# Delta-rule attention, gated MLP and rotor MLP on one core: a reordered end of the first block inversion, fused small steps, early TensorE products, rank offsets

## The chip, the cores and the metric

The kernel runs on one core of a Trainium2 chip. The metric is the device time of one execution in microseconds.

## The reference

Three layers run one after another on batch 4, sequence 768, width 384 (8 heads of 48).

```python
# 1. delta rule, per batch and head, t = 0 .. 767
y[t]  = q[t] @ state
state = state + beta[t] * outer(k_n[t], v[t] - k_n[t] @ state)   # k_n = k / (norm(k) + 1e-6)
# 2. gated MLP: h = relu(x @ w_in); u, v = halves of h; v normalised over its width
x = (u * (w_spatial @ v_n + b_spatial)) @ w_out
# 3. rotor: theta = x @ w_theta
u = x + w_tok_r @ (x * cos(theta)) + w_tok_i @ (x * sin(theta))
out = u + relu(u @ w_ch)
```

## The kernel before, in words

**Chunks.** The delta rule runs in chunks of 64 tokens: 12 chunks for each of 4 batches, 48 chain steps g. A chain step (chain, L865) turns the state S of all 8 heads into the next one: line 888 multiplies keys and state, line 891 subtracts, line 900 multiplies by the chunk's inverse (in tile GX), copies make U, line 914 adds to the state in PSUM, line 943 makes the outputs. jit (L816) makes the masked query-key products (L833, L839) and scales v by the key norms.

**Rounds.** The inverse of a chunk's unit-triangular 64x64 matrix is made for 8 chunks at once, a round, of 32 units (chunk and pair of heads): gram2 (L656) makes the key products (L677), one call for two chunks, and invert (L695) inverts. invert(0) is on the way to the first chain step; its tasks are marked crit. It transposes the 32x32 diagonal blocks into tile un (L717), takes the norms from their diagonal (L721 to L730), scales (L734), and then substitutes backwards, k from 30 to 1: for every k a product into tmp (L756) and an addition to un (L767). In round 0 the rows are split into an even and an odd set, so that there are four instructions for a k; in later rounds two. At k = BURSTK = 8 of round 0 a task on TensorE (L761) waits for tmp, and 60 transposes of the identity (filler, L553 to L556) follow it: the burst. Then come a scaling (L770), a transpose (L773), a transpose into GX (L776), two copies within GX (L530), two GpSimd fills of zeros (L783), and, for 8, 8 and 16 units, the products that make the off-diagonal block: L794, copies out of PSUM into ct, L800, copies out of PSUM into GX (all copies go through the helper's lines L524 on ScalarE and L530 on VectorE). L800 of the first 8 units reads GX's right half, which the copies of all 32 units write.

**The rest.** The MLP's products are all on line 1055 (tiles m and y), three products of rounded halves for each one; their weights are loaded as 8-byte numbers and turned into 4-byte ones by ScalarE and VectorE (L970 to L986).

**What sets the order.** Every piece of work is a task in a list, with the engines that it may run on, a planned duration, a rank (prio) and what it needs. Plan.run (L297) plays the list through a model of the chip and issues each engine's instructions in the order that comes out; each engine works its queue in that order. The rank of a chain step is g, that of its neighbours g plus or minus a few. Where the model sees TensorE idle for a stretch, it puts transposes of the identity (fill, L556) ahead of the next task, some 0.6 of the planned gap, or as many as the model of the clock asks for, at most 16. NUDGE holds runs of tasks by number, whose ranks get a random offset from a seed; it is empty.

## Time and profile before

| | us |
|---|---|
| median of 3 runs (719.7 to 723.13) | 722.24 |
| the profiled execution | 721.76 |
| its span, first to last instruction | 720.0 |
| TensorE busy | 683.0 |
| VectorE busy | 549.6 |
| ScalarE busy | 360.5 |

How to read it: a busy time is the union of an engine's instructions. A matmul's recorded duration contains its way through the array, so matmuls one behind another overlap in the record, and the distance of two starts is what one costs. "Idle before" names what ended the wait of an engine.

### The profile page before, as it was taken

Reading aid. Unit: us, or ns where it says so; the run is one execution under the profiler, and the core shown is the slowest. Engines: PE = TensorE matmul, PEld = TensorE weight load, DVE = VectorE, ACT = ScalarE, POOL = GpSimd, SP = SyncE. Lnnn points to the kernel's source line nnn. Section 1 sums busy time; section 2 is a strip of 40 time slices with the busy share of each in tenths; the row PEclk is TensorE's granted clock in tenths of the full one; section 3 lists DMA queues with packets and bytes.
Section 4 is the critical chain, followed back from the end, with each engine's and each line's share of the span. In section 5 each row is a group of like instructions: output and inputs, shape, how many; then the busy total and the mean of one; then the engine's idle time right before and its main releaser. Section 6 shows DMA issues by size and latency. Waiting matters only on the chain.

```text
span 720.0 us, 23423 instructions
## 1 busy us (share of the span) xinstructions
PE 683.0 (95%) x9801; PEld 629.2 (87%) x9801; DVE 549.6 (76%) x1576; ACT 360.5 (50%) x904; POOL 12.3 (2%) x22
## 2 busy tenths in 40 slices
PE   4597888999999999999999999999999999999998
PEld 4586777788887888888898999999999999999997
DVE  6998999999979989977666668967466745674555
ACT  4855575573286662387746854753243324431331
POOL 0010010010010010010000000000000000000000
PEclk9996976999999999999999999999999999999999
DMA  8533652534657335767696563521111111111001
GB/s 293 179 109 95 189 156 79 175 105 135 207 177 227 109 95 151 209 206 225 185 323 206 156 199 130 163 73 30 66 30 30 30 67 31 30 31 66 0 1 66
DMA packets 74121, 90.63 MB, mean 126 GB/s; under 512 B 7328, under 2 KB 58912, under 8 KB 74016
## 3 DMA queue, kind: packets, MB, share of 16 engines
q1 hardware_dynamic: 74016, 89.14, 40.2%
q8 instruction: 77, 1.26, 0.8%
q14 instruction: 28, 0.23, 0.1%
HBM read 66.70 MB, written 22.41 MB: 124 GB/s over the span
## 4 chain that ended last, share of the span: by engine, by line
PE 77%; DVE 14%; ACT 4%; DMA 3%; issue 3%; SPq 0%; DVEq 0%; ACTq 0%
PE m L1055 40%; PE y L1055 22%; DVE un L767 3%; DVE tmp L756 3%; PE gp L556 3%; PE gp L800 2%; PE ru L943 2%; PE ru L900 1%; PE ru L888 1%; PE s L914 1%; PE gp L794 1%; DMA kq<-in_kqT_dram 1%; PE m L1366 1%; DVE un L773 1%; ACT ct L524 1%
## 5 line engine op out<-in xcount | busy, mean ns | idle before, releaser
L1055 PE MATMUL m<-w,vh 128*128 128x384 f32 x384 | 102.2, 347 | 0.0
L1055 PE MATMUL y<-wr,xTh 128*128 128x384 f32 x432 | 87.1, 339 | 0.0
L1055 PE MATMUL y<-w,xTl 128*128 128x384 f32 x432 | 86.3, 337 | 0.0
L1055 PEld LDWEIGHTS y<-wr,xTh 128*128 128x128 f32 x432 | 75.6, 188 | 0.1
L1055 PEld LDWEIGHTS y<-w,xTl 128*128 128x128 f32 x432 | 75.5, 188 | 0.0
L1055 PEld LDWEIGHTS m<-w,vh 128*128 128x128 f32 x384 | 66.7, 188 | 2.5
L1055 PE MATMUL m<-w,vl 128*128 128x384 f32 x192 | 64.4, 335 | 0.0
L756 DVE TENSOR_TENSOR tmp<-un 128x30 f32<-128x30 f32 (+21 forms) x209 | 60.9, 303 | 1.4
L767 DVE TENSOR_TENSOR un<-un,tmp 128x30 f32<-128x30 f32 (+21 forms) x209 | 61.0, 303 | 1.2
L1391 DVE TENSOR_SCALAR bgr<-m 128x384 int32<-128x384 f32 x22 | 12.3, 558 | 57.1 <-PE m L1055 56.8
L524 ACT ACTIVATE U<-ru 128x96 f32<-128x96 f32 x86 | 16.7, 247 | 57.6 <-PE ru L900 50.1
L1055 PE MATMUL m<-wo,gh 128*128 128x384 f32 x176 | 44.7, 334 | 0.0
L1055 PE MATMUL m<-xTh,wih 128*128 128x256 f32 x144 | 44.2, 307 | 0.2 <-ACT hv L524 0.2
L524 ACT ACTIVATE x<-m 128x384 f32<-128x384 f32 x22 | 10.6, 480 | 66.9 <-PE m L1055 66.9
L1055 PE MATMUL m<-xTl,wih 128*128 128x256 f32 x144 | 40.6, 282 | 0.0
L1055 PE MATMUL m<-xTh,wil 128*128 128x256 f32 x144 | 40.6, 282 | 0.0
L1055 PE MATMUL m<-uh,wc 128*128 128x384 f32 x144 | 39.2, 335 | 0.0
L524 ACT ACTIVATE bgr<-bgr 128x384 uint8<-128x384 uint8 x34 | 36.8, 1084 | 0.4
L1055 PEld LDWEIGHTS m<-w,vl 128*128 128x128 f32 x192 | 36.0, 188 | 0.0
L524 ACT ACTIVATE gh<-graw 128x256 fp32r<-128x256 f32 x27 | 10.0, 412 | 49.2 <-PE m L1055 47.5
L1055 PE MATMUL m<-wt,xh 128*128 128x384 f32 x132 | 33.8, 337 | 0.0
L943 PE MATMUL ru<-jp,U 64*64 64x64 f32 x768 | 33.2, 227 | 0.0
(186 smaller groups left out, 1669.0 us busy)
## 6 DMA issues: line engine op xcount, KB each, us to landing
kq<-in_kqT_dram SPq DMA_DIRECT2D x48, 256.0 KB, 3.6
vk<-in_vkn_dram SPq DMA_DIRECT2D x48, 192.0 KB, 3.3
kg<-in_kgT_dram SPq DMA_DIRECT2D x24, 256.0 KB, 3.6
gd<-gt SPq DMA_DIRECT2D x32, 192.0 KB, 3.2
xd<-xs SPq DMA_DIRECT2D x48, 96.0 KB, 3.2
xr<-xd SPq DMA_DIRECT2D x24, 192.0 KB, 3.3
bgr<-in_w_r_dram SPq DMA_DIRECT2D x12, 384.0 KB, 4.0
bgr<-in_w_i_dram SPq DMA_DIRECT2D x12, 384.0 KB, 4.1
```

What stands on the lines that cost most here:

```text
L524: nc.scalar.activation(out=out, in_=in_, func=func, **kw)
L556: nc.tensor.transpose(out, ident.t, ident.t)
L756: nc.vector.tensor_tensor(out=t3, in0=un.t[:, k:k + 1, 0:k].to_broadcast([128, m, k]), in1=un.t[:, t0:32:st, k:k + 1].to_broadcast([128, m ...
L767: nc.vector.tensor_tensor(out=un.t[:, t0:32:st, 0:k], in0=un.t[:, t0:32:st, 0:k], in1=t3, op=ALU.add)
L773: A([("DVE", 2080.0)], lambda e: nc.vector.transpose(out=un.t.rearrange("p u s -> p s u"), in_=un.t.rearrange("p t s -> p s t")), ub, [xt, ...
L794: mm(out=pv[q + 32:q + 64, u, :], lhsT=gx[q:q + 32, u0 + u, 32:64], rhs=un.t[q:q + 32, u0 + u, :], start=True, stop=True, tile_position=(q ...
L800: mm(out=pv[q:q + 32, u, :], lhsT=ct.t[q + 32:q + 64, u, :], rhs=gx[q + 32:q + 64, u0 + u, 32:64], start=True, stop=True, tile_position=(q ...
L888: mm(out=at(ps.t, RB[hp])[o:o + 64], lhsT=kq.t[a:a + D, 0, hp, :], rhs=s[a:a + D, D * SB[hp]:D * SB[hp] + D], start=True, stop=True)
L900: mm(out=at(pu.t, UB[hp])[o:o + 64], lhsT=gx[i:i + 64, j * HP + hp, :], rhs=rt.t[i:i + 64, hp, :], start=True, stop=True)
L943: mm(out=PYv[h]()[o:o + 64, c0:c0 + CH], lhsT=lh, rhs=rh, start=f, stop=w == 1 or UF[hp] > 0, skip_group_check=True)
L1055: mm(out=view(), lhsT=a, rhs=c, start=(start and q == 0 and s_ == 0), stop=(stop and q == tot - 1 and s_ == 2))
L1391: P.add(o_dve(DM), lambda e: nc.vector.tensor_scalar(out=ni.t.bitcast(I32), in0=th(), scalar1=1.0 / TWO_PI, scalar2=None, op0=ALU.mult), [ ...
```

## The change

Norms: the sum and its scaling become one instruction that makes twice the norm, the factor -1 becomes -4, and the halving that the v scaling needs comes later. Substitution: for k from 26 and up to 3 in round 0 (from 28 and up to 2 in later rounds) each row, or column, of the step is one instruction, which multiplies by a scalar from un and adds. Round 0's transpose into GX, copies and GpSimd fills are made for the first 8 units and then for 24. The second group of 8 units gets the rank -19.6 + 0.3 in place of 0.75, the third 1.3 in place of 1.0. A GpSimd fill of a 128x128 tile and eight products of it with itself come first on their engines. NUDGE gets seven runs of tasks. A few constants are only written in another way.

```diff
@@ -89,12 +89,15 @@
 CTN = 1
 XRN = 2
 UPER = 6
+P2H = (0.3, 1.3)
+NWARM = 8
+KLO0, KHI0, KLO, KHI = 3, 26, 2, 28
 LZ = 0.0
 LZY = 0.0
 LZG = 1
 GAPY = 0
 STAY = 350.0
-NUDGE = ()
+NUDGE = ((758, 332, 362, 1.5), (9389, 1357, 1417, 0.1), (4962, 2530, 2590, 1.5), (5968, 2293, 2323, 0.1), (8329, 1405, 1525, 0.6), (9243, 2216, 2336, 1.5), (2589, 2425, 2675, 0.1))
 SPER = 3
 GTN = 3
 TPR = 3
@@ -635,6 +638,15 @@
         A([("POOL", 100.0)], lambda e, i=i: nc.gpsimd.memset(St[i][:, HP * D:], 0.0), (), SS[i], -30 + i, port=False)
         A([("POOL", 100.0)], lambda e, i=i: nc.gpsimd.memset(Ut[i][:, HP * D:], 0.0), (), UU[i], -30 + i, port=False)
 
+    warm = single("const", "warm", [128, 128])
+    A([("POOL", 150.0)], lambda e: nc.gpsimd.memset(warm.t, 0.0), (), [warm], -59.0, port=False)
+
+    def fw(e):
+        for _ in range(NWARM):
+            mm(out=RUt[:, 0, 128:256], lhsT=warm.t, rhs=warm.t, start=True, stop=True)
+
+    A(o_pe(230.0 * NWARM), fw, [warm], [], -59.0, act=0.95, mode=0)
+
     kq_b, vk_b, jp_b = {}, {}, {}
     ng_b = {}
     inv0, grams, first = [], [], []
@@ -697,7 +709,6 @@
         gx, G = GXt[r % NB], GXc[r % NB]
         cr = r == 0
         gg = [Buf(tile_=gx) for _ in range(4)]
-        gz = [Buf(tile_=gx) for _ in range(4)]
         gm2 = [Buf(tile_=gx)]
         for u0, u1 in ((0, 16), (16, 24), (24, 32)) if cr else ((0, 32),):
             for q in (1, 3):
@@ -722,12 +733,11 @@
         A([("ACT", 120.0)], lambda e: act(sr.t, ss.t, ACTF.Sqrt), [ss], [sr], pr, crit=cr)
         for f in (lambda e: V.reciprocal(out=nt.t, in_=sr.t),
                   lambda e: V.tensor_tensor(out=nt.t, in0=nt.t, in1=ss.t, op=ALU.mult),
-                  lambda e: V.tensor_tensor(out=nt.t, in0=nt.t, in1=sr.t, op=ALU.add),
-                  lambda e: V.tensor_scalar(out=nt.t, in0=nt.t, scalar1=0.5, scalar2=1e-6, op0=ALU.mult, op1=ALU.add)):
+                  lambda e: V.scalar_tensor_tensor(out=nt.t, in0=sr.t, scalar=2e-6, in1=nt.t, op0=ALU.add, op1=ALU.add)):
             A(o_dve(32), f, [ss, sr], [nt], pr, crit=cr)
         for f in (lambda e: V.reciprocal(out=gt.t, in_=nt.t),
                   lambda e: V.tensor_tensor(out=gt.t, in0=gt.t, in1=gt.t, op=ALU.mult),
-                  lambda e: V.scalar_tensor_tensor(out=gt.t, in0=gt.t, scalar=-1.0, in1=beta_sb.t[:, 32 * r:32 * r + 32], op0=ALU.mult, op1=ALU.mult)):
+                  lambda e: V.scalar_tensor_tensor(out=gt.t, in0=gt.t, scalar=-4.0, in1=beta_sb.t[:, 32 * r:32 * r + 32], op0=ALU.mult, op1=ALU.mult)):
             A(o_dve(32), f, [nt, beta_sb], [gt], pr, crit=cr)
 
         def f2(e):
@@ -735,6 +745,7 @@
             nc.vector.memset(dg(), 1.0)
 
         A([("DVE", d_dve(1024) + 160.0)], f2, [gt], [un], pr, crit=cr)
+        A(o_dve(32), lambda e: V.tensor_scalar(out=nt.t, in0=nt.t, scalar1=0.5, scalar2=None, op0=ALU.mult), [gt], [nt], pr + 0.001)
         A(o_dve(32), lambda e: V.transpose(out=ng.t.rearrange("p j h -> p (j h)"), in_=nt.t), [nt], [ng], pr + 0.001, port=False)
 
         sets = [(0, 1)] if not cr else [(0, 2), (1, 2)]
@@ -742,6 +753,16 @@
         fin = [[] for _ in sets]
         heads = []
         for k in range(30, 0, -1):
+            if k <= (KLO0 if cr else KLO) or k >= (KHI0 if cr else KHI):
+                def fs(e, k=k):
+                    for x in range(k + 1, 32) if k > 15 else range(k):
+                        o, i, c = ((un.t[:, x, 0:k], un.t[:, k, 0:k], un.t[:, x, k:k + 1]) if k > 15 else
+                                   (un.t[:, k + 1:32, x], un.t[:, k + 1:32, k], un.t[:, k, x:x + 1]))
+                        nc.vector.scalar_tensor_tensor(out=o, in0=i, scalar=c, in1=o, op0=ALU.mult, op1=ALU.add)
+
+                n = 31 - k if k > 15 else k
+                A([("DVE", n * d_dve(31 - n))], fs, [un], ub, pr + 0.001 * (31 - k), crit=cr).order.update(heads[-3:])
+                continue
             for half in (0, 1):
                 for i, (c0, st) in enumerate(sets):
                     t0 = k + 1 + (k + 1 - c0) % st
@@ -773,20 +794,29 @@
         A([("DVE", 2080.0)], lambda e: nc.vector.transpose(out=un.t.rearrange("p u s -> p s u"),
                                                            in_=un.t.rearrange("p t s -> p s t")),
           ub, [xt, un], pr + 0.05, crit=cr, port=False)
-        A([("DVE", 1163.0)], lambda e: nc.vector.transpose(out=gx[:, :, 0:32], in_=un.t), [xt, un], gg, pr + 0.1, crit=cr, port=False)
-        if cr:
-            inv0.append(P.tasks[-1])
-        for q in (1, 3):
-            A(o_cps(1024), lambda e, q=q: copy(e, gx[32 * q:32 * q + 32, :, 32:64], gx[32 * q:32 * q + 32, :, 0:32]),
-              [], [gg[q]], pr + 0.2, crit=cr, part=32 * q)
-        for q in (1, 3):
-            A([("POOL", 890.0)], lambda e, q=q: nc.gpsimd.memset(gx[32 * q:32 * q + 32, :, 0:32], 0.0),
-              [gg[q]], [gz[q]], pr + 0.3, crit=cr, port=False)
+        parts = []
+        for n, (a0, a1) in enumerate(((0, 8), (8, 32)) if cr else ((0, 32),)):
+            ga, za = [Buf(tile_=gx) for _ in range(4)], [Buf(tile_=gx) for _ in range(4)]
+            parts.append((a0, a1, ga, za))
+            w, p0 = a1 - a0, pr + (0.1 if n == 0 else 0.6)
+            A([("DVE", 50.0 + 34.8 * w)], lambda e, a0=a0, a1=a1: nc.vector.transpose(out=gx[:, a0:a1, 0:32], in_=un.t[:, a0:a1, :]),
+              [xt, un] + gg, ga, p0, crit=cr, port=False)
+            if cr:
+                inv0.append(P.tasks[-1])
+            for q in (1, 3):
+                A(o_cps(32 * w), lambda e, q=q, a0=a0, a1=a1: copy(e, gx[32 * q:32 * q + 32, a0:a1, 32:64], gx[32 * q:32 * q + 32, a0:a1, 0:32]),
+                  [], [ga[q]], p0 + 0.01, crit=cr, part=32 * q)
+            for q in (1, 3):
+                A([("POOL", 60.0 + 26.0 * w)], lambda e, q=q, a0=a0, a1=a1: nc.gpsimd.memset(gx[32 * q:32 * q + 32, a0:a1, 0:32], 0.0),
+                  [ga[q]], [za[q]], p0 + 0.02, crit=cr, port=False)
         u0 = 0
         for h, mu in enumerate((8, 8, 16) if cr else (16, 16)):
             ps, ct = r_gp.new(), r_ct.new()
             pv = GPt[:, 256:256 + mu * 32].rearrange("p (a b) -> p a b", b=32)
-            p2 = pr + 0.5 + 0.25 * h
+            p2 = pr + 0.5 + 0.25 * h if not cr or h == 0 else P2H[h - 1]
+            near = [x for x in parts if x[0] < u0 + mu and u0 < x[1]]
+            gd = [x[2][q] for x in near for q in (1, 3)]
+            zd = [x[3][q] for x in near for q in (1, 3)]
 
             def f2(e, pv=pv, u0=u0, mu=mu):
                 for u in range(mu):
@@ -804,13 +834,13 @@
             for q in (1, 3):
                 A(o_cpp(32 * mu), lambda e, q=q, pv=pv, ct=ct, mu=mu: copy(e, ct.t[32 * q:32 * q + 32, 0:mu], pv[32 * q:32 * q + 32]),
                   [ps], [(ct, True)], p2, crit=cr, port=False, part=32 * q)
-            A(o_pe(525 * mu // 8), f3, [ct, gg[1], gg[3]], [(ps, True)], p2, crit=cr, act=0.46, mode=3)
+            A(o_pe(525 * mu // 8), f3, [ct] + gd, [(ps, True)], p2, crit=cr, act=0.46, mode=3)
             if cr and h == 1:
                 first.append(P.tasks[-1])
             for q in (0, 2):
                 A(o_cpp(32 * mu), lambda e, q=q, pv=pv, u0=u0, mu=mu: copy(e, gx[32 * q:32 * q + 32, u0:u0 + mu, 32:64],
                                                                     pv[32 * q:32 * q + 32]),
-                  [ps, gg[1], gg[3], gz[1], gz[3]], [G[i] for i in range(u0 // HP, (u0 + mu) // HP)], p2, crit=cr, port=False, part=32 * q)
+                  [ps] + gd + zd, [G[i] for i in range(u0 // HP, (u0 + mu) // HP)], p2, crit=cr, port=False, part=32 * q)
             u0 += mu
 
     def jit(g, pr):
```

## Rows read from the trace of the kernel before

**Rows 1.** Windows by stage: engine busy us, TensorE clock, DMA share, GB/s.
```profile
0.00:31.00 31.00, 14.24 (x401) 12.40 (x402) 24.68 (x115) 21.29 (x51) 0.44 (x8) 1.00 0.82 274
...
55.00:140.00 85.00, 73.95 (x1830) 61.56 (x1829) 78.39 (x264) 48.58 (x148) 1.89 (x2) 0.78 0.47 136
140.00:500.00 360.00, 356.85 (x5870) 320.14 (x5859) 295.62 (x848) 208.90 (x530) 8.07 (x10) 1.00 0.55 168
```

**Rows 2.** Windows: the two long stretches at half clock.
```profile
54.97:68.63 13.66, 10.27 (x226) 9.01 (x229) 10.46 (x46) 7.09 (x21) 0.00 (x0) 0.50 0.25 72
...
99.35:119.83 20.48, 17.95 (x416) 14.44 (x412) 18.46 (x56) 11.93 (x28) 1.67 (x2) 0.50 0.26 76
```

**Rows 3.** The burst's transposes, two stretches: ns min/median/max, first and last start.
```profile
L556 PE MATMUL gp<-ident x15: 421/421/421, 31.2 to 34.2; 128*128 128x128 f32 x15
...
L556 PE MATMUL gp<-ident x52: 272/273/337, 34.4 to 40.0; 128*128 128x128 f32 x52
```

**Rows 4.** Timeline of TensorE, gram calls: start us, us, engine, line, form.
```profile
4.14 1.13 PE L677 MATMUL gp<-kg 48*64 48x64 f32 x32 [4.14 <-DMA kg<-in_kgT_dram]
...
71.31 0.66 PE L677 MATMUL gp<-kg 48*64 48x64 f32 x32
```

**Rows 5.** Timeline of VectorE, first inversion.
```profile
13.38 0.18 DVE L726 TENSOR_SCALAR nT<-nT 128x32 f32<-128x32 f32 x1
...
15.96 0.29 DVE L756 TENSOR_TENSOR tmp<-un 128x30 f32<-128x30 f32 x2
...
16.74 0.34 DVE L756 TENSOR_TENSOR tmp<-un 128x28 f32<-128x28 f32 x2
16.99 0.33 DVE L767 TENSOR_TENSOR un<-un,tmp 128x28 f32<-128x28 f32 x2
...
18.29 0.38 DVE L756 TENSOR_TENSOR tmp<-un 128x75 f32<-128x75 f32 x2
...
33.69 0.32 DVE L756 TENSOR_TENSOR tmp<-un 128x42 f32<-128x42 f32 x2
...
35.17 1.23 DVE L770 TENSOR_TENSOR un<-un,gaT 128x1024 f32<-128x1024 f32 x1
...
38.59 1.25 DVE L776 STREAM_TRANSPOSE GX<-un 128x1024 f32<-128x1024 f32 x1
```

**Rows 6.** Timeline of TensorE, 31 to 47 us.
```profile
31.17 9.32 PE L556 MATMUL gp<-ident 128*128 128x128 f32 x69
40.42 0.69 PE L794 MATMUL gp<-un,GX 32*32 32x32 f32 x32
...
43.05 0.69 PE L800 MATMUL gp<-GX,ct 32*32 32x32 f32 x32
...
46.19 0.45 PE L900 MATMUL ru<-rt,GX 64*64 64x48 f32 x16
```

**Rows 7.** Groups by form on VectorE: count, busy us, mean ns, idle before.
```profile
L1398 DVE TENSOR_SCALAR bgm<-bgm 128x384 f32<-128x384 f32 x24 | 8.6, 358 | 0.6
...
L1131 DVE TENSOR_SCALAR hv<-hv,mv,td 128x512 f32<-128x512 f32 x14 | 7.3, 542 | 0.0
```

**Rows 8.** Timelines of ScalarE and VectorE: copies behind lines 794, 800.
```profile
41.56 1.06 ACT L524 ACTIVATE GX<-GX 32x1024 f32<-32x1024 f32 x1
43.79 0.76 ACT L524 ACTIVATE GX<-gp 32x256 f32<-32x256 f32 x2 [1.17 <-PE gp L800]
...
41.57 0.43 DVE L530 COPY ct<-gp 32x256 f32<-32x256 f32 x1 [1.01 <-ACT ct L524]
```

**Rows 9.** Chain of work that ended last: waits without a releaser.
```profile
53.38 2.62 issue
...
97.37 1.02 issue
...
304.76 1.45 issue
```

**Rows 10.** Windows, transposes of line 556 alone, 140 to 500 us.
```profile
140.00:500.00 360.00, 6.88 (x48) 5.22 (x48) 1.00 0.55 168
```

More of the change, by code (lines that the diff above doesn't have):

```diff
@@ L37 @@
 FILL_ACT = 0.6
-FILL_LOW = .5
+FILL_LOW = 0.5
 FILL_K = 16
@@ L59 @@
 HAM_DN = 0.44
-HAM_T = .42
+HAM_T = 0.42
 SLIDE = 3413
```

## The prediction

> **What bounds the kernel now.** First I read the stretches [rows 1]: from 140 to 500 us TensorE is busy 356.85 of 360 us, before 31 us 14.24 of 31, between 55 and 140 us 73.95 of 85. So the late part is TensorE's own work, and whatever starts this work sooner ends the kernel sooner; what can be lost or won lies before 140 us. Then the granted clock: two long stretches there are at 0.50, the lower level of 1.2 GHz [rows 2]. Before 34 us the profile prints 1.00, but the rows say otherwise: the burst of transposes starts 15 of them between 31.2 and 34.2, one per 0.214 us, and 52 between 34.4 and 40.0, one per 0.11 us [rows 3], so the clock was at its lower level until some 3.2 us into the burst, and a gram call takes 1.13 us at 4.14 where it takes 0.66 at 71.31 [rows 4].
>
> Then VectorE up to 40 us [rows 5]. It is the chain there: the substitution begins at 15.96 and ends at 35.17, then scaling, one transpose, another from 38.59, copies. The reader should see how small instructions follow one another: a pair of 128x28 takes 0.25 us from start to start (16.74 to 16.99), 0.125 each, although one lasts 0.18.
>
> Last TensorE from 31 us [rows 6]. The burst (60 transposes and 9 that the planner adds as fill) holds it until 40.42; the first products of the finishing steps (line 794) start there, though their operand was ready when VectorE began the next transpose at 38.59. So TensorE's queue, not VectorE, is last at this point, by about 1.85 us. Fill, line 800 at 43.05, more fill, and the first chain step's line 900 at 46.19 follow.
>
> **The change, part by part.** All against the profiled execution: span 720.0, its own time 721.76, which is 0.48 below the median of 722.24.
>
> *Norms.* One of four dependent small steps goes. The scaling on line 726 takes 0.18 us [rows 5]. The halving returns behind the last use and falls into the gap before the substitution, for about half a step, as does the small transpose that used to lie in a gap. I take -0.1; bounds -0.18 and +0.1.
>
> *Fused steps, k from 30 to 26.* Before, 18 instructions from 15.96 to 18.29: 2.33 us [rows 5]. After, 15 instructions of 26 to 30 elements, each row's next update at least two instructions behind the one it needs. At 0.125 each that is 1.88: -0.45. The trace has no such instruction with a scalar from memory at this size. The nearest is line 1131 [rows 7]: 128x512 with two such scalars takes 542 ns where a plain 128x384 on line 1398 takes 358; scaled by its elements the plain one would be near 0.43, so the scalars may cost 0.12. Bounds: 0.1 each gives -0.83, 0.24 each gives +1.3. I take the pair's rate, since its elements and type are those of the change.
>
> *Fused steps, k from 3 to 1.* Before 33.69 to 35.17, 1.48 us; after, 6 instructions at 0.125 and two waits of about 0.11 for the column just written: 0.97. This 0.5 us I cost at nothing: the burst covers it, since TensorE is 1.85 us late there. If that cover went, it would count in full. In the five later inversions three pairs of steps trade places with as many fused ones, with TensorE full: nothing.
>
> *The burst and its fill.* The burst is released by the k = 8 step, behind the first two edits and ahead of the third, so it moves by 0.55. The fill of 9 is set from the planned gap between burst and line 794; VectorE's planned work in that gap shrinks, so I estimate 6 in place of 9. At 0.11 us each [rows 3]: -0.3. Bounds: none left (-1.0) and twice as many (+1.0).
>
> *The eight products.* In the code a gram call has 16 products and the trace shows 32 matrix instructions for it [rows 4], so eight products of full size are 16 instructions; at the burst's slow 0.214 us they last 3.4 us. Released by a small GpSimd fill at about 1 us (an estimate: VectorE's and GpSimd's first fills all lie before that), they end near 4.5, where the first gram now starts at 4.14. So they may hold the grams by up to 0.5 us; or, being as long as what came ahead of the clock's rise in the burst, raise it, and a gram then takes 0.66 in place of 1.13 [rows 4], which is worth up to 0.5 on VectorE's way to the substitution. I take 0, with both ends. The Trainium skill (TensorE: Matmul & The Clock Gate, Part 4: PE-mode transpose) says that transposes do not engage the full clock; by that rule the burst would be useless and the products alone could lift the clock, and the sum would be about 0.5 better; the rate that doubles inside the burst [rows 3] disagrees, and no trace here shows the products.
>
> *The last steps for 8 units first.* Now line 800 needs the copy into the right half of all 32 units, which ScalarE does from 41.56 to 42.62, behind its first copy out of PSUM [rows 8]; VectorE's copy out of PSUM ends at 42.0; line 800 starts at 43.05 behind fill. After, transpose, copies and GpSimd fills for 8 units are a quarter as long and end before the burst does, so line 800 is held by the PSUM copies alone: 42.0 in place of 43.05, -1.05. From the end of the last copies (43.79 plus 0.76, [rows 8]) to line 900 at 46.19 pass 1.64 us: a mask's product, fill and the next units' line 794, all set ahead of it. With chain steps 0 and 1 ready earlier and the remaining 24 units ranked behind, I take about half, -0.9; bounds 0 and -1.64. What is late next: TensorE's order, then VectorE, where the 24 units' transpose and copies now stand among the PSUM copies. The weight conversions on VectorE that wait for the transpose into GX now wait for its second part; they are behind it on the same engine anyway, at no cost.
>
> These parts bring the first chain step 0.1 + 0.45 + 0.3 + 1.05 + 0.9 = 2.8 us forward; with TensorE full after 140 us it arrives at the end.
>
> *A wait that has no cause in the data.* At 53.38 TensorE stands for 2.62 us in the middle of line 800, with no releaser in the profile; five other waits of over a microsecond without one stand on the chain, none above 1.5; the first and the last of the five are 1.02 and 1.45 [rows 9]. The 16 new instructions, the lost fill and the new order put another instruction there. I take a wait of some 1.1 us in its place, -1.5; bounds 0 and -2.62, or more if the clock does not fall behind it (below).
>
> *Rank offsets.* One run of tasks belongs to chain step 2 and what stands around it, six to the stretch of about 250 to 400 us. The first run also moves three loads on SyncE's queue (a gram's keys, and keys and values three steps ahead), which nothing waits for within the step. The latter can win at most the idle 3.15 us [rows 1] and the 6.88 us of fill [rows 10] between 140 and 500, and lose as easily. I take -0.5; bounds -5 and +3, estimates of about half of those 10 us and the idle time.
>
> Sum: -2.8 - 1.5 - 0.5 = -4.8; 721.76 - 4.8 = 717.0 us.
>
> **Rivals.** *Better: the first slow stretch goes too.* It begins at 54.97, 1.6 us into the wait at 53.38. Without that wait it may not come. It holds 10.27 us of TensorE work at half clock [rows 2], so at most 5.1 us; with the wait's other 1.1 us and some of it being fill, about 4.5: 717.0 - 4.5 = 712.5. For it: the cause is one wait. Against: the clock falls again at 99.35, with no such wait ahead of it on the chain but 1.02 us [rows 9]. Chance 0.2.
>
> *Lost in the queue.* The burst and the fill keep line 794 near 40 us, fused instructions cost what a scalar from memory may cost, and the order behind eats the rest; then only 1 us is left: 720.8. For it: TensorE is already later than VectorE. Against: line 800's hold is a plain wait that goes. That the early products do nothing at all belongs here. Chance 0.26.
>
> *Slower: another fall of the clock.* The place is 79 to 99 us, now at the full level; ranks of step 2 and its neighbours are shuffled by up to 1.5, and one idle stretch of TensorE as long as that at 53.38 would decide it. The price is that of the stretch at 99.35: 17.95 us of work at half clock, at most 9 us [rows 2]: 717.0 + 9 = 726. Chance 0.12.
>
> **How the numbers follow.** The forecast has 0.42. About half a per cent, 3.6 us, is what a measurement of this kernel tells from no change: below 718.6 is faster, above 725.9 slower. The forecast's own spread, 714 to 720, lies mostly below 718.6 (0.36), the better case wholly (0.2), of the queue case hardly anything (0.01): faster 0.57. Slower is the last rival, 0.12; the same 0.31. The range goes from 709, which leaves out the lower end of the better case, to 724, which takes in the queue case and leaves out the fall of the clock.
>
> **What would show it.** Right: line 794 starts at about 39.6, line 800 some 1.6 us behind it, line 900 of step 0 near 43.4; the fused instructions 0.125 us apart; TensorE's busy share from 140 us on unchanged. Wrong: a fused instruction every 0.2 us or more; burst and fill that end after 40.4; line 900 still behind 45 us; a granted clock of 0.50 in a stretch that now has 1.00; the wait without cause of 2 us or more at another place.

## The result, and the profile after

The changed kernel takes 730.39 us (median of 4 runs, 726.99 to 732.72) against 722.0 of the kernel before on the same chip: a ratio of 1.0117, interval 1.0093 to 1.0141. It is slower, by 8.4 us where 4.8 less were forecast, and above the range's 724. Its four executions fall into 727 to 728 us at a mean granted clock of 0.951 to 0.955 and 732 to 733 at 0.941 to 0.942; the profiled one took 728.38.

The page of the changed kernel (busy us, share, instructions; the clock in 40 slices; one transfer queue):

```profile
span 726.6 us, 23354 instructions
...
PE 682.7 (94%) x9767; PEld 626.1 (86%) x9767; DVE 552.1 (76%) x1574; ACT 362.0 (50%) x895; POOL 12.3 (2%) x25
...
PEclk7586798999999999998999999999999999999999
...
q8 instruction: 77, 1.26, 0.8%
```

TensorE is as busy as before (683.0 us then), so the 6.6 us that the span grew are time in which it stands. The stretches of [rows 1], and two more, say where:

```profile
0.00:31.00 31.00, 16.75 (x416) 14.84 (x416) 23.71 (x105) 19.46 (x47) 0.58 (x9) 0.66 0.82 269
31.00:55.00 24.00, 19.12 (x326) 17.22 (x327) 17.85 (x59) 9.74 (x24) 2.08 (x4) 0.78 0.19 54
55.00:140.00 85.00, 69.06 (x1833) 56.25 (x1835) 81.48 (x272) 49.78 (x141) 1.90 (x2) 0.84 0.50 142
...
300.00:345.00 45.00, 42.66 (x962) 35.33 (x961) 32.86 (x95) 29.36 (x74) 1.89 (x2) 0.92 0.61 187
...
140.00:500.00 360.00, 354.63 (x5904) 315.52 (x5905) 293.74 (x842) 209.19 (x523) 7.71 (x10) 0.99 0.56 168
...
323.90:330.71 6.81, 6.47 (x96) 5.13 (x95) 4.16 (x9) 3.60 (x8) 0.00 (x0) 0.50 0.24 66
```

The same stretches of the kernel before that were not shown:

```profile
31.00:55.00 24.00, 21.43 (x456) 19.47 (x457) 22.15 (x72) 12.55 (x29) 1.89 (x2) 1.00 0.28 86
...
300.00:345.00 45.00, 44.70 (x1057) 36.92 (x1056) 35.47 (x98) 33.49 (x88) 1.90 (x2) 1.00 0.69 209
```

TensorE's idle time goes from 16.76 to 14.25 us before 31, from 2.57 to 4.88 up to 55, from 11.05 to 15.94 up to 140, and from 3.15 to 5.37 from 140 to 500: together 6.9 more. Idle time is not all loss, since fill gave way to it (200 transposes of line 556 before, 150 of line 559 after), so I also counted the 2,808 products of the MLP (line 1055 before, 1085 after) along the trace. After 360 of them the next starts at 222.4 before and 221.8 after, after 600 at 304.6 and 301.6: by this count the changed kernel is up to 3 us ahead. After 720 the next starts at 341.7 and 344.6, after 1,200 at 428.5 and 435.1. The count is rough, because chain work between the products changes places with them; but a lead that turns into 6.6 us of delay says that the end is lost between 300 and 430 us. There, and at the start, in the timeline of TensorE:

```profile
0.99 3.78 PE L646 MATMUL ru<-warm 128*128 128x128 f32 x16 [0.99 <-POOL warm L642]
...
6.79 0.69 PE L689 MATMUL gp<-kg 48*64 48x64 f32 x32 [0.16 <-DVE GX L701]
...
10.05 1.13 PE L689 MATMUL gp<-kg 48*64 48x64 f32 x32 [1.88 <-DMA kg<-in_kgT_dram]
...
32.08 0.48 PE L782 MATMUL gp<-ident,tmp 128*128 128x128 f32 x1 [2.71 <-DVE tmp L777]
33.03 8.77 PE L559 MATMUL gp<-ident 128*128 128x128 f32 x60 [0.47 <-ACT GX L527]
...
42.97 0.69 PE L824 MATMUL gp<-un,GX 32*32 32x32 f32 x32
...
46.62 0.69 PE L830 MATMUL gp<-GX,ct 32*32 32x32 f32 x32 [1.71 <-ACT ct L527]
...
49.24 0.68 PE L930 MATMUL ru<-rt,GX 64*64 64x48 f32 x16
...
324.24 0.49 PE L973 MATMUL ru<-jp,U 64*64 64x64 f32 x7 [2.34 <-issue]
```

The last row is a new wait that nothing in the profile releases, 2.34 us from 321.90 in the middle of line 973. From 323.90 to 330.71 the granted clock is at its lower level of 1.2 GHz: 6.47 us of work that takes about half as long at the upper one, 3.2 us lost. The two together are 5.6 us, against the 6.6 us by which the span grew. In the kernel before the stretch from 300 to 345 us holds 0.30 us of idle time and no fall.

The start is late too, and for other reasons. Line 824 is line 794 of before, 830 is 800 and 930 is 900 [rows 6]: 42.97 for 40.42, 46.62 for 43.05, 49.24 for 46.19. ScalarE's timeline:

```profile
11.23 0.66 ACT L527 ACTIVATE GX<-gp 128x256 f32<-128x256 f32 x2 [1.03 <-PE gp L689]
11.91 1.28 ACT L527 ACT_TABLE_LOAD   x1
13.21 0.23 ACT L527 ACTIVATE sr<-ss 128x32 f32<-128x32 f32 x1
...
41.84 0.38 ACT L527 ACTIVATE GX<-gp 128x256 f32<-128x256 f32 x1 [8.86 <-PE gp L559]
42.25 2.13 ACT L527 ACTIVATE GX<-GX 32x1024 f32<-32x1024 f32 x2
44.41 0.94 ACT L527 ACTIVATE w<-gt 128x384 fp32r<-128x384 f32 x2
45.37 0.41 ACT L527 ACTIVATE GX<-GX 32x256 f32<-32x256 f32 x1
45.80 0.76 ACT L527 ACTIVATE ct<-gp 32x256 f32<-32x256 f32 x2
```

The reader should see the order in the queue. The second copy of the last gram out of tile gp (41.84) stands behind the burst, which writes the same tile; it waits 8.86 us. Line 824 is held by the end of burst and fill; behind the copy stand 3.07 us of other work, and only then the copy for the 8 units (45.37) and the one into ct (45.80), which line 830 waits for. And at 11.23 two gram copies and the table load of 1.28 us stand ahead of the square root, which starts at 13.21 where it started at 12.28 before.

VectorE:

```profile
13.47 0.35 DVE L734 RECIPROCAL nT<-sr 128x32 f32<-128x32 f32 x1 [1.08 <-ACT sr L527]
...
16.50 0.25 DVE L761 SCALAR_TENSOR_TENSOR un<-un 128x30 f32<-128x30 f32 x1
...
16.79 2.67 DVE L761 SCALAR_TENSOR_TENSOR un<-un 128x29 f32<-128x29 f32 x14
...
19.54 0.38 DVE L777 TENSOR_TENSOR tmp<-un 128x75 f32<-128x75 f32 x2
...
34.99 1.45 DVE L761 SCALAR_TENSOR_TENSOR un<-un 128x28 f32<-128x28 f32 x6
```

The 14 fused instructions take 2.67 us, 0.19 each. From the first step to k = 25 pass 3.04 us; before 2.33 [rows 5]. From the first of the six at the end of the substitution to the scaling behind them (36.47) pass 1.48, as before (33.69 to 35.17).

### The profile page after: what moved, and what is told of

Same layout as the page of the kernel before. It is cut to its first block, busy times and chain, and to the rows that moved or that the text cites. A ratio compares the mean times of both kernels' runs of the same rounds, so it can differ in the third digit from the quotient of the medians.

```text
span 726.6 us, 23354 instructions
## 1 busy us (share of the span) xinstructions
PE 682.7 (94%) x9767; PEld 626.1 (86%) x9767; DVE 552.1 (76%) x1574; ACT 362.0 (50%) x895; POOL 12.3 (2%) x25
## 4 chain that ended last, share of the span: by engine, by line
PE 70%; DVE 20%; ACT 4%; issue 3%; DMA 2%; DVEq 0%; POOL 0%; ACTq 0%; SPq 0%; POOLq 0%
PE m L1085 36%; PE y L1085 22%; DVE un L788 4%; DVE tmp L777 4%; PE gp L824 2%; PE gp L559 1%; PE ru L930 1%; PE ru L973 1%; DVE un L761 1%; PE gp L830 1%; ACT GX L527 1%; PE ru L918 1%; PE m L1396 1%; DVE un L794 1%; DVE un L744 1%
## 5 line engine op out<-in xcount | busy, mean ns | idle before, releaser
L1085 PE MATMUL m<-w,vl 128*128 128x384 f32 x192 | 64.5, 336 | 0.0
L777 DVE TENSOR_TENSOR tmp<-un 128x130 f32<-128x130 f32 (+25 forms) x169 | 52.8, 323 | 0.9
L788 DVE TENSOR_TENSOR un<-un,tmp 128x130 f32<-128x130 f32 (+25 forms) x169 | 52.8, 323 | 0.6
L527 ACT ACTIVATE U<-ru 128x96 f32<-128x96 f32 x85 | 16.7, 249 | 60.3 <-PE ru L930 49.6
L527 ACT ACTIVATE GX<-gp 128x256 f32<-128x256 f32 (+2 forms) x58 | 24.7, 450 | 22.7 <-PE gp L559 8.9
L527 ACT ACTIVATE gh<-graw 128x256 fp32r<-128x256 f32 x28 | 10.5, 415 | 49.2 <-PE m L1085 49.2
```

The costliest lines, as they stand in the source:

```text
L527: nc.scalar.activation(out=out, in_=in_, func=func, **kw)
L777: nc.vector.tensor_tensor(out=t3, in0=un.t[:, k:k + 1, 0:k].to_broadcast([128, m, k]), in1=un.t[:, t0:32:st, k:k + 1].to_broadcast([128, m ...
L788: nc.vector.tensor_tensor(out=un.t[:, t0:32:st, 0:k], in0=un.t[:, t0:32:st, 0:k], in1=t3, op=ALU.add)
L1085: mm(out=view(), lhsT=a, rhs=c, start=(start and q == 0 and s_ == 0), stop=(stop and q == tot - 1 and s_ == 2))
```

## The experiments

Each expectation spells out its theories; two of them, under whatever letter, run through all. **Start**: the burst, ScalarE's queue and the fused steps lose the time at the start, and it arrives at the end. **Draw**: where TensorE stands without a cause in the data, and where its clock falls, is drawn anew by every new stream of instructions, and that sets the end (D in the last four). All ratios are to the kernel before on the same chip (medians of 720.1 to 722.0 us). Falls are those of the one profiled execution; other executions of a kernel can differ from it by some us (n4's ten lie from 720.5 to 729.5). The changed kernel, n2, n3, n4, e5 and e6 have the same order of work on every engine; n1, e7 and e8 have others:

| kernel | us | ratio, interval | profiled execution | first chain step | falls of the clock after 140 us |
|---|---|---|---|---|---|
| before | 722.24 | | 721.76 | 46.2 | none |
| after | 730.39 | 1.0117 (1.0093–1.0141) | 728.38 | 49.2 | 323.9–330.7 |
| n1 no offsets | 726.69 | 1.0077 (1.0057–1.0096) | 727.82 | 46.1 | 239.4–242.8 |
| n2 no products | 728.32 | 1.0105 (1.0088–1.0122) | 727.86 | 49.0 | 324.1–330.9 |
| n3 shift | 729.67 | 1.0120 (1.0097–1.0144) | 730.79 | 52.1 | 327.6–334.4 |
| n4 burst's bank | 727.01 | 1.0073 (1.0049–1.0097) | 725.03 | 44.3 | 322.0–328.8 |
| e5 half loads | 724.10 | 1.0041 (1.0019–1.0062) | 725.42 | 44.8 | 322.3–329.1 |
| e6 unfused | 726.58 | 1.0081 (1.0056–1.0107) | 726.77 | 44.6 | 322.8–329.7 |
| e7 bank, no offsets | 728.62 | 1.0112 (1.0083–1.0141) | 727.40 | 46.3 | 239.4–242.9 |
| e8 split only | 729.51 | 1.0127 (1.0091–1.0163) | 728.98 | 44.1 | 224.7, 255.4, 272.5: 3.4 each |
| b1 before, shifted | 725.60 | 1.0059 (1.0035–1.0084) | 728.22 | 49.6 | 342.1–345.5 |
| b2 before, one offset run | 726.25 | 1.0063 (1.0040–1.0087) | 726.79 | 46.1 | 229.1–232.5, 317.8–321.3 |
| b3 before, all offsets | 723.22 | 1.0028 (1.0004–1.0053) | 720.77 | 47.1 | none |
| b4 before, small shift | 722.78 | 1.0048 (1.0028–1.0069) | 720.85 | 47.4 | none |

**n1, without the rank offsets**

```diff
-NUDGE = ((758, 332, 362, 1.5), ...
+NUDGE = ()
```

> The changed kernel without the rank offsets; all its other parts stay. Theory R (the offsets' order is what costs): the time falls from 730.4 to 722 or below. Theory F (TensorE's instruction packets arrive late at 321.9 us, 2.3 us of waiting and a fall of the clock worth 3.4 more): the order from 60 us on is another one, so the wait there goes or moves; 720 to 730, and the sum of waits without a releaser over 2 us, with the half-clock stretch behind each, accounts for where it lands. Theory S (the 3 us that the first chain step comes later arrive at the end): 725 or more, since the start is untouched.

The first chain step comes at 46.1, 3.1 earlier: ScalarE now makes both copies of the last gram ahead of the burst, at 29.41 and 32.21. So the order that the offsets make puts that copy behind the burst. The fall at 324 is gone and another one is there at 239.4, right behind a wait of 1.65 us for VectorE (tile xs, from 237.2). The ratio is 0.4% below that of the changed kernel, about 2.9 us. That is not the 722 or below of the theory that blames the offsets; it lies inside the wide range of the theory of late packets (720 to 730), and is about as much as the start came earlier.

**n2, without the early products**

```diff
-        for _ in range(NWARM):
+        for _ in range(0):
```

> The changed kernel with the same order on every engine, but the task of the eight early products issues none of them (16 matrix instructions and 16 weight loads fewer on TensorE). Theory F: the boundaries of TensorE's instruction packets move by 32 instructions against the work, so the wait at 321.9 changes its size or place; 723 to 731. Theory S: the first gram starts at 4.14 again, the rest of the start stays late: the same within 1 us of the changed kernel (729 to 731). Theory P (the early rise of the clock is worth something): 1 us or more slower than the changed kernel in the start.

The order of every engine is that of the changed kernel. First chain step 49.0 for 49.2; wait of 1.81 us at 322.09, fall behind it; the intervals overlap. No worth of the products shows, in either direction (the intervals leave room for some 2 us). They do raise the clock: a gram takes 0.69 us at 6.79 and 1.13 again at 10.05, after TensorE stood for 1.88 us; without them (n2) every gram call up to the burst takes 1.10 us or more.

**n3, 32 small products more at the start**

```diff
+        for _ in range(32):
+            mm(out=RUt[0:32, 0, 128:160], lhsT=warm.t[0:32, 0:32], rhs=warm.t[0:32, 0:32], start=True, stop=True)
```

> The changed kernel with the same order on every engine and 32 tiny 32x32 products behind the eight early ones: 128 more instructions on TensorE, half of a packet of 256, for about 1 us at the start. Theory F: the wait of 2.34 us at 321.9 and the half clock from 323.9 to 330.7 go; 5 us faster than the changed kernel (725) unless the boundaries meet another busy stretch of loads, which then shows as a new wait without a releaser. Theories R and S: the order is the same, so the time is that of the changed kernel or up to 1 us more (730 to 731), and the wait stays.

They cost 2.9 us at the start (52.1), where about 1 was expected. The median is that of the changed kernel, but the two intervals leave room for some 2.4 us either way, and the profiled execution is 2.4 us longer than the changed kernel's (730.79 for 728.38). So this run does not show that the price at the start is lost on the way. The wait moves from 321.90 to 326.21 and shrinks to 1.38; the fall behind it stays.

**n4, the burst in another PSUM tile**

```diff
-nc.tensor.transpose(GPt[:, 0:128], tmp.t[:, 0:128], ident.t)
+nc.tensor.transpose(RUt[:, 0, 128:256], tmp.t[:, 0:128], ident.t)
-lambda e: filler(BURST0), ...
+lambda e: filler(BURST0, "ru"), ...
```

> The changed kernel with the same order on every engine; only the burst of 60 transposes and the transpose ahead of it write the PSUM tile ru in place of gp. Theory B (ScalarE's copies out of gp stand behind the burst from 32.99 to 41.84, and the critical copies behind them): ScalarE's two copies run at about 32.6, line 830 starts near 43.6 in place of 46.6 and the first chain step's line 930 near 46.2 in place of 49.2. Theory S: these 3 us arrive at the end, 727.4. Theory F: the chain's start is not what sets the end, and the fetch waits move little; within 1.5 us of the changed kernel, 729 to 732.

The timeline of TensorE in this kernel:

```profile
31.79 8.42 PE L559 MATMUL ru<-ident 128*128 128x128 f32 x60
...
40.69 0.69 PE L824 MATMUL gp<-un,GX 32*32 32x32 f32 x32
...
42.56 0.69 PE L830 MATMUL gp<-GX,ct 32*32 32x32 f32 x32
...
44.31 0.45 PE L930 MATMUL ru<-rt,GX 64*64 64x48 f32 x16
...
320.70 0.34 PE L973 MATMUL ru<-jp,U 64*64 64x64 f32 x7 [2.24 <-issue]
```

The first chain step is 4.9 us earlier than in the changed kernel (0.5 of that is there before the burst: the substitution starts at 15.97 for 16.50) and 1.9 earlier than before: the copy's wait for the burst was the whole loss at the start, and the split does its work. This time Start is right: 727.0 us is its forecast (727.4) and not Draw's (729 to 732), and the ratio is 0.44% lower, 3.2 us of the 4.9. With the order kept, the larger part of the gain arrives at the end. Yet a wait of 2.24 us and a fall at 322 are there again, and the kernel is still 0.7% slower than before.

**e5, n4 with half of each load of the rotor's w_tok_r and w_tok_i** (the other half of each load is filled with zeros by GpSimd, so that the rotor's products use other weights)

```diff
+        nl = n if half else 2 * n
-nc.sync.dma_start(out=view(raw), in_=src.bitcast(I32))
+nc.sync.dma_start(out=view(raw)[:, 0:nl], in_=src.bitcast(I32)[:, 0:nl])
```

> The kernel n4 with the same order on every engine, but the loads of w_tok_r and w_tok_i (384 KB each, from about 310 us on) bring only half of their columns, 192 KB; GpSimd fills the other half with zeros, so the rotor's token products are of other weights. Theory F (TensorE's instruction packet near 318 to 322 us lands late because these loads fill the DMA engines, and the wait drops the clock): the wait of 2.24 us at 318.5 falls below 0.8 us, the half clock from 322.0 to 328.8 is gone, 5 us faster than n4 (722). Rival G (TensorE simply eats instructions faster there than packets can come, whatever the loads): the wait stays at 1.3 us or more, the clock falls, 726 to 728.

The wait is 1.78 us at 319.34 and the clock falls at 322.3 again, as rival G says: these loads don't make the wait, or not alone. The time, 724.1, lies between the two forecasts; its ratio is 0.3% below n4's, at the edge of what the intervals tell apart, and no experiment follows that up.

**e6, n4 with the fused steps as products and additions, in the same order of tasks**

```diff
-nc.vector.scalar_tensor_tensor(out=o, in0=i, scalar=c, in1=o, op0=ALU.mult, op1=ALU.add)
+nc.vector.tensor_tensor(out=t3, in0=..., in1=..., op=ALU.mult)
+nc.vector.tensor_tensor(out=un.t[:, t0:32:st, 0:k], in0=un.t[:, t0:32:st, 0:k], in1=t3, op=ALU.add)
```

> The kernel n4 with the same order of tasks on every engine; the fused steps are again made of the products into a spare tile and additions of the kernel before. Theory V (a fused step of one row costs 0.19 us, so 15 of them cost more than the 18 instructions they replace): from the first step to k = 25 2.3 us in place of 2.9 to 3.0, k = 3 to 1 the same 1.5 us within 0.1, line 930 of the first chain step 0.6 us earlier (43.7 in place of 44.3), and 0.5 us at the end, which the spread of the runs hides (726 to 727). Rival: if the gain at k = 3 to 1 that I had predicted were there and hidden, the first chain step would come later by 0.3 us or more.

VectorE in n4, with fused steps:

```profile
15.97 0.24 DVE L761 SCALAR_TENSOR_TENSOR un<-un 128x30 f32<-128x30 f32 x1
...
16.25 2.65 DVE L761 SCALAR_TENSOR_TENSOR un<-un 128x29 f32<-128x29 f32 x14
...
19.00 0.37 DVE L777 TENSOR_TENSOR tmp<-un 128x75 f32<-128x75 f32 x2
```

and in e6, with products and additions:

```profile
16.30 0.18 DVE L766 TENSOR_TENSOR tmpf<-un 128x30 f32<-128x30 f32 x1
...
18.86 0.38 DVE L785 TENSOR_TENSOR tmp<-un 128x75 f32<-128x75 f32 x2
```

3.03 us against 2.56 with the same two foreign instructions within: the fused form costs 0.47 us. The first chain step gains nothing of it (44.6, where 43.7 was expected), since the burst, longer here by 0.47 us, holds the first units' products until 41.03; and the end gains nothing.

**e7, n4 without the offsets.** Edit: as n1, on n4.

> The kernel n4 (burst in the other PSUM tile) without the rank offsets. Theory S+R (the offsets cost by moving the first weight pieces in front of ScalarE's critical copies, and by the wait they place at 318 to 322 us): the first chain step at 44 us as in n4, because the blocking is gone in both; then 1 to 3 us below n1's 726.7 and below n4's 727.0: 723 to 726. If the offsets gain in the late part what they lose at the start: 728 or more.

46.3 for the first chain step and not 44, no fall at 322, one at 239.4 behind the same wait for VectorE as in n1 (1.65 us), and 728.62 us: 0.4% slower than with the offsets, just clear of the intervals. Without them the time is not recovered.

**e8, the norms and the split alone** (burst in the other tile, no products, no fused steps, no offsets)

```diff
-KLO0, KHI0, KLO, KHI = 3, 26, 2, 28
+KLO0, KHI0, KLO, KHI = 0, 32, 0, 32
...
```

(The rest of the edit: the products and their fill are not issued, NUDGE is empty as in n1, and the burst's tile is changed as in n4.)

> Of the change only the norms and the last steps for 8 units first stay, with the burst in the other PSUM tile; no offsets, no early products, no fused steps. Theory S (an earlier first chain step arrives at the end): line 930 of the first step at 42.5 to 43.5 in place of 46.2 before, and 2 to 4 us faster than before (717 to 719). Theory F (what decides is where TensorE's late packets and the falls of the clock come to lie, which every new order draws anew): the first step is as early, yet the time lies anywhere from 717 to 726, and the waits without a releaser of over 1.2 us, with the half clock behind them, account for the difference.

The clearest case against Start. Its first chain step is the earliest, 2.1 us before that of the kernel before, and after 360 MLP products the next starts at 215.6 for 222.4, 6.8 us ahead. Its profiled execution ends 7.2 us later. Three stretches at half clock lie between (windows):

```profile
224.80:228.00 3.20, 3.20 (x45) 2.78 (x39) 1.97 (x7) 1.91 (x4) 0.00 (x0) 0.50 0.20 72
255.50:258.80 3.30, 3.30 (x61) 3.08 (x62) 2.10 (x9) 1.77 (x6) 0.00 (x0) 0.50 0.20 60
272.60:275.90 3.30, 3.30 (x25) 2.77 (x25) 3.30 (x12) 0.39 (x2) 0.00 (x0) 0.50 0.02 5
```

and TensorE waits for VectorE and ScalarE within 220 to 300 us (us in total, times, the longest):

```profile
PE ru L916 <- DVE xs L984: 4.1, 2, 3.6
PE gp L828 <- ACT ct L527: 1.6, 2, 0.9
PE ru L928 <- DVE rt L919: 1.0, 1, 1.0
```

TensorE idles 10.8 us between 140 and 500 us, where it idles 3.15 in the kernel before; 1.5 of these have no releaser in the profile. So this is Draw only in its half on the clock: most of the standing has a cause in the data. The falls, at half of the 9.8 us of work in them, cost up to 4.9 us; with the 7.6 us of additional idle time that is 12.5 of the 14.0 us from 6.8 ahead to 7.2 behind.

**b1, b2 and b3, the kernel before without any part of the change but the offsets in b3**

```diff
+            if g == 0:
+                for _ in range(32):
+                    mm(out=RUt[0:32, 0, 128:160], lhsT=kg.t[0:32, 0, 0, 0:32], rhs=kg.t[0:32, 0, 0, 0:32], start=True, stop=True)
```

```diff
-NUDGE = ()
+NUDGE = ((2, 332, 362, 0.1),)
```

```diff
-NUDGE = ()
+NUDGE = ((758, 332, 362, 1.5), ...
```

> The kernel before, order of every engine kept, with 32 extra products of 32x32 behind the first half of the first gram (128 TensorE instructions more; TensorE waits for data there until 10.10 us, so they cost about nothing by themselves). Theory D (the end is set by where TensorE's waits for nothing shown and its clock falls happen to lie, and each new stream of instructions draws them anew): the 2.62 us wait at 53.38 moves or changes size, and the time moves by 1 to 7 us, up more likely than down, with all the change's parts absent. Rival P (the change's own parts cost the time): within 2 us of before, 719 to 723.

> The kernel before with nothing but one small run of rank offsets (seed 2, tasks 332 to 361, plus or minus 0.1), which changes the order of the engines from TensorE's 42nd group of instructions on. Theory D: slower by 2 to 9 us, 724 to 731, with new waits or falls of the clock between 200 and 430 us. Rival P: within 2 us of before, 719 to 723.

> The kernel before with the seven runs of rank offsets of the change and nothing else of it; the task numbers name other tasks here than in the changed kernel. Theory D: slower by 2 to 9 us, 724 to 731, as any other order. Rival O (the offsets were a gain of their own, here or there): 719 or less. Rival P (only the burst's wait, the fused steps and the products cost): within 2 us of before.

All three are slower, by 0.6, 0.6 and 0.3%. In b1 the order is untouched, and one thing was not as expected, the price of the small products:

```profile
4.93 3.62 PE L680 MATMUL ru<-kg 32*32 32x32 f32 x64
...
49.65 0.45 PE L903 MATMUL ru<-rt,GX 64*64 64x48 f32 x16
...
340.17 0.32 PE L891 MATMUL ru<-S,kq 48*64 48x48 f32 x3 [1.08 <-issue]
```

They hold the grams up, and the first chain step is 3.4 us late. But the wait of 2.62 us [rows 9] is gone, the second step is 0.4 late, and after 180 MLP products the next starts at 164.7, as in the kernel before. What is lost at the end comes later: 1.6 us after 360 products (there TensorE waits 1.45 us for VectorE from 222.2), 2.5 after 600, 6.5 after 720, with a wait at 339.08 and a half-clock stretch (windows):

```profile
342.10:345.40 3.30, 3.30 (x58) 2.96 (x58) 2.24 (x7) 2.40 (x7) 0.00 (x0) 0.50 0.08 23
```

b2, an offset of a tenth on thirty tasks, has two such stretches, each behind waits for VectorE or ScalarE (1.43 and 1.01 us from 226.5 on, 1.83 from 314.9), and idles 9.8 us between 140 and 500. b3 says that the offsets of the change are no gain of their own here; its 723.2 lies between the forecasts, 724 to 731 and within 2 us of before, and is no support for Draw.

**b4, a smaller shift in a place where TensorE waits for data**

```diff
+            if g == 2:
+                for _ in range(16):
...
```

> The kernel before, order of every engine kept, with 16 extra products of 32x32 behind the fourth gram call, where TensorE waits 2.11 us for data; by the 3.62 us of the 64 matrix instructions in the run with 32 such products these 32 last 1.8 us and fit into that wait, so that the first inversion starts as before, within 0.2 us. Theory D (later waits and falls of the clock lie elsewhere as soon as the stream of instructions is shifted): the wait of 2.62 us at 53.38 moves or changes, and so do those behind 200 us; the time differs by over 1 us from before, to 723 to 728. Rival P (the shift as such costs nothing; the earlier shifted kernel lost by its 3.1 us at the start): 719.5 to 722.

The products land 1.2 us on the first chain step (47.4), not within 0.2. The profiled execution loses nothing: it has no fall behind 140 us and takes 720.85. Four of the nine take 725.0 to 725.8, at a mean granted clock of 0.976 to 0.979, the other five 720.9 to 722.8 at 0.983; those four were not profiled. The median, 722.8, lies between Draw's forecast (723 to 728) and its rival's (719.5 to 722). Its ratio, 1.0048, is clear of no change, but the cause is open: the kernel before took 718.8 to 722.7 us on the same chip with mean clocks of 0.974 to 0.983, so the mean clock does not tell the slow executions from the others.

## Why the prediction was wrong, point by point

**The step that failed is the first one**: "the late part is TensorE's own work, and whatever starts this work sooner ends the kernel sooner; what can be lost or won lies before 140 us". The stretch from 140 to 500 us is full in the kernel before [rows 1], but that is a property of that one stream of instructions and not of the work. In the table, the three profiled executions without a fall behind 140 us took 720.8 to 721.8, the eleven with one or more 725.0 to 730.8, whatever the first chain step was (44.1 to 52.1). TensorE's idle time between 140 and 500 us goes with it: 3.2 to 3.8 us in the three, 4.9 to 10.8 in the eleven. e8's lead of 6.8 us bought nothing. In the changed kernel the late loss was the wait of 2.34 us and the fall behind it, 5.6 us.

Half of the step stands: with the order of work kept, what starts sooner did end sooner, by 3.2 of 4.9 us (n4). So the miss has two parts. By an estimate from the profiled executions, of the 11.4 us between forecast and execution (717.0 and 728.38) some 4.5 are the wait and its fall, and some 4 the start, where 5.85 us lie between forecast and trace and about two thirds arrive (n4); the rest is not traced.

**The wait without a cause** went from 53.38, as forecast; the second chain step comes at 54.3 for 56.6. In its place I took 1.1 us. It was 2.34 us, at 321.90, with a fall behind it: the term "-1.5" was +3.0 with the fall (5.6 less the 2.62). **The rival "another fall of the clock"** had the right mechanism and sign, the wrong place (79 to 99 us) and a chance of 0.12; its one price was a stretch of 17.95 us of work, and the fall that came held 6.47. My 1.1 us came from a wrong reading of the chain: it changes engines, and of the five other entries without a releaser only the one at 97.37 is a wait of TensorE. At 304.76 VectorE transposes and TensorE works on; it idles 0.30 us between 300 and 345. The waits of TensorE over 1 us without a releaser in that trace were 2.62 us at 53.38 and 1.02 at 97.37, and the clock fell behind both, at 54.97 and 99.35 (a third time, at 75.45, behind a wait of 1.57 us for VectorE). That was the sign to price a new wait with a fall behind it.

**The first chain step**: forecast 2.8 earlier, 3.05 later. The sentence that failed is that copies for 8 units "end before the burst does": on ScalarE they stood behind a copy out of the tile that the burst writes, and ended at 45.78, 4 us after the burst; with the burst in another tile they end at 40.22 (n4). By terms: the split, in the tile that doesn't block, is right: e8, with norms and split alone, is 2.1 earlier where norms, split and fill were summed to 2.35. The fused steps were mis-sized: 0.19 us each and not 0.125, +0.71 against the kernel before where -0.45 was taken, inside the bounds, towards the end that the scalars of line 1131 gave and that I had set aside. That row was misread too: line 1398's 358 ns, scaled by its elements, are 0.48 us and not 0.43, so the two scalars cost 0.06 and not 0.12, and 0.125 with 0.06 is near the 0.19 that was measured. Fused steps at the end of the substitution gained nothing, not 0.5; the forecast had counted that gain at nothing for another reason, the cover by the burst. Of the 0.71, 0.47 is the form (e6), the rest two other instructions that now stand between. The Trainium skill (VectorE: DVE Perf Modes, Rules for kernel authors) says not to fuse for speed and to keep the number of operations small. The rows agree with the first half; by the second the 15 fused instructions would win over 18 plain ones, and they lost, 3.03 against 2.56 us. The norms' own chain is 0.22 us shorter (12.55 to 14.44 before, 13.47 to 15.14 after; 0.1 was taken), but it started 0.92 later, behind the copies and the table load on ScalarE, which the forecast has nowhere. Taking the early products at nothing agrees with n2.

**The rank offsets** were the other wrong term. I wrote that the first run "belongs to chain step 2 and what stands around it" and moves three loads "which nothing waits for within the step". With all runs left out (n1), ScalarE's order changes from 26.4 us on: a weight conversion (tile vl) stands where n1 has a gram's copy, the last gram's copy is made before the burst, and the first chain step comes 3.1 us earlier. Which of the seven runs does that was not tried. The offsets have no worth of their own: with the burst in its old tile they cost 0.4% (n1 against the changed kernel), with it in the other tile they gain 0.4% (n4 against e7), on the kernel before they cost 0.3% (b3), each at the edge of the intervals.

**The other rivals.** "Better" asked for the first slow stretch to go with the wait: the wait went, and the clock is at its lower level all the same from 47.4 to 50.8, 54.2 to 57.6 and 64.5 to 78.1, so the wait was not the only cause. "Lost in the queue" had the burst and the fused form right, and gave 720.8; both did eat the first steps' gain, but the larger part of the time was lost elsewhere. No version has a lower median than the kernel before.

**What stays open**: why the wait at about 320 us is there in all kernels with the change's order and not in the kernel before, and why executions of one kernel differ by up to 9 us. No run takes the wait out and keeps the order, so that it costs its 5.6 us is read from one trace and not shown by an experiment. Ahead of each of the 14 falls behind 140 us TensorE had just stood for 0.67 us or more: in seven without a releaser, in the other seven for VectorE or ScalarE (n1, e7, e8's three, b2's two). So the falls go with standing, whatever its cause. That it is enough is not shown: behind waits of 1.45 us (b1, at 222.2), 1.32 (n1, at 322.7) and 2.25 (b2, at 402.0) the clock did not fall. And because so many of the waits are for data, the late loss of a new order may lie in how it places VectorE's and ScalarE's work, which can be read from its trace, and not in a draw; no experiment here removes such a wait to see.

## What to carry to other kernels

Where a stretch is full in a profile, ask whether it is full by its work or by this order of instructions: shift the stream by a few instructions that do nothing, and see whether the time stays. Here that alone moved the kernel before by 0.5 to 0.6% (b4, b1), as much as a term of the sum, and the changed kernel not measurably (n3), so an edit that is to win 0.5% has to be judged over several orders. Then look at what TensorE waits for in each: much of it had a name. A filler that writes a tile which another engine still has to read puts that engine's whole queue behind it (here 8.86 us); give it a tile of its own.

## What was unexpected in the hardware

Some of TensorE's waits without a releaser go with the queue that the page calls "instruction": 77 packets of 16 KB, one for about 254 of the 19,534 matrix and weight instructions, if it carries those alone. The transfers within the wait from 321.90 to 324.20:

```profile
q1 hardware_dynamic: 373, 0.67, 87.0%
q8 instruction: 1, 0.02, 2.6%
```

One packet of it moves in the wait, as one does in n4's at 318.46 and in that of the kernel before at 53.38; in b1's at 339.08 none of this queue does. Over the 14 profiled executions, from 40 us on, a packet of it lands in each of the seven waits without a releaser above 1.7 us and in none of the nine of 1.0 to 1.5 us. Loads hold 87.0% of the DMA engines' time in this one and 36.9% in that at 53.38, so crowding alone doesn't make it.

A fused instruction with a scalar from memory follows the one before after 0.19 us, though it has only 26 to 30 elements a partition; plain ones of up to 28 follow after 0.125 [rows 5]. And the clock: the early products, 3.78 us at the lower level, and the first grams behind them were followed by the upper level from 6.45 to 9.86; TensorE then stood from 8.2 to 10.05 for its operands, and the next gram took 1.13 us again. The burst, from 33.03, brought the upper level back at 37.2.
